# Keys by four heads with both signs, partly DMA-transposed LN1 and one-input statistics in a conditioned linear-attention block

## Chip, cores and metric

The kernel runs on one core of one Trainium2 chip. The metric is the device time of one execution in microseconds (us); every ratio here uses runs of the fast state alone. The runs come from three chips, so across chips the ratio to the kernel before on the same chip is the safer comparison. PE is the matrix engine (TensorE), DVE VectorE, ACT ScalarE, POOL GpSimd, SP the engine that issues most DMAs. LN1 and LN2 are the two layer norms.

## The reference

2048 tokens of width 512 pass a conditioned layer norm, linear attention with 32 heads of width 16, whose features are two softmaxes (of the projected vector and of its negative), and then a second layer norm and a gated MLP (F = 1376).

```python
mod = (silu(c) @ w_mod).reshape(1, 6, 1, -1)              # sa, ca, ga, sb, cb, gb
h = layernorm(x) * (1 + ca) + sa
q, k, v = split(h @ wqkv)                                  # 32 heads of 16
pq, pk = q @ w_phi, k @ w_phi                              # per head, 16x16
phi_q = concat(softmax(pq), softmax(-pq))                  # 32 features per head
phi_k = concat(softmax(pk), softmax(-pk))
kv = einsum('bhsf,bhsd->bhfd', phi_k, v);  z = phi_k.sum(tokens)
o = (phi_q @ kv) / (phi_q @ z + 1e-6)
x = x + ga * (o @ wo)
h = layernorm(x) * (1 + cb) + sb
x = x + gb * ((sigmoid(h @ w_gate) * (h @ w_up)) @ w_down)
```

## The kernel before

Tokens come in 16 tiles of 128. The kernel has its own list scheduler: each piece of work names its engines, buffers, a due time and sometimes a release time, and the schedule is computed when the kernel is built. The due times are hand-set constants.

LN1, with `mv1` holding mean and variance, `rs1` the reciprocal deviation and `nmr` = -mean x rs1:

```python
# two inputs in SBUF: mean and rs of 1 or 2 tiles at once
dve.scalar_tensor_tensor(nmr[:, 0, sl], mv1[:, sl, 0], -1.0, rs1[:, sl], op0=ALU.mult, op1=ALU.mult)
...
def f_xn(e, t=t, xn=xn):                       # normalize one tile, on the engine that the scheduler chose
    if e == "ACT":
        act.activation(xn[:], x_sb[:, t, :], ACT.Identity, scale=rs1[:, t:t + 1], bias=nmr[:, 0, t:t + 1])
    elif e == "DVE":
        dve.tensor_scalar(xn[:], x_sb[:, t, :], mv1[:, t, 0:1], rs1[:, t:t + 1], op0=ALU.subtract, op1=ALU.mult)
    else:
        pool.tensor_scalar(xn[:], x_sb[:, t, :], rs1[:, t:t + 1], nmr[:, 0, t:t + 1], op0=ALU.mult, op1=ALU.add)
...
pe.transpose(tp[:, tl * P:(tl + 1) * P], xn[:, j * P:(j + 1) * P], ident[:])   # 64 of these
dve.tensor_scalar(dst, tp[:], modc[:, 4 + j:5 + j], modc[:, j:j + 1], op0=ALU.mult, op1=ALU.add)  # or ACT: h1T
```

The key/value stage, per tile: K and V on PE, two exponentials on ACT (`e`), sums and reciprocals (`ks`, DVE or ACT), `phi` = e x 1/sum on POOL, the cast of V to `vaug` on ACT, then the sum over tokens:

```python
for g in range(NG):                            # 8 groups: one sign, 8 heads, 136 columns
    s, blk = g // 4, g % 4
    pe.matmul(acc[g // 3][:, (g % 3) * 136:(g % 3) * 136 + 136],
              lhsT=ph[...][:, s, blk * 8:(blk + 1) * 8, :], rhs=vaug[va.slot][:, blk * 8:(blk + 1) * 8, :], ...)
```

At the end of the stage, DVE multiplies the sums by a block mask into `kvbd`. The queries, output projection, LN2 and MLP follow.

Of the kernel before, what the change touches and what calls it, by code (L numbers as in the profile page):

```python
# [10 lines left out]
BF16 = mybir.dt.bfloat16  # L11
# [18 lines left out]
SPLIT = 14  # L30
T0, KP, GL = 11.57, 2.64, 7.92
WARM = [3.5, 3.8, 4.1, 4.4, 4.7, 5.0, 5.3, 5.6, 5.9, 6.2, 7.0, 7.6, 8.2, 8.8, 9.4, 10.0]
LG = [[0], [1], [2, 3], [4, 5], [6, 7], [8, 9], [10, 11], [12, 13], [14, 15]]
QREL = [43.49, 61.34, 57.73, 11.53]
AREL = [-41.36, 49.26, 40.7, 68.7, 71.54, 83.02, 104.54, 113.86, 145.92]
RS1 = [{"ACT": 0.4}] * 3 + [{"POOL": 1.1, "ACT": 0.4}] * 6
XN1 = [
    ['ACT'], ['ACT', 'DVE'], ['ACT'], ['ACT', 'POOL'], ['POOL'], ['DVE', 'ACT', 'POOL'], ['POOL', 'DVE', 'ACT'], ['ACT'], ['DVE'],
    ['POOL', 'DVE'], ['POOL', 'DVE'], ['DVE', 'POOL'], ['DVE', 'ACT'], ['POOL'], ['ACT', 'POOL'], ['ACT', 'DVE', 'POOL'],
# [3 lines left out]
    [['DVE', 'ACT'], ['DVE'], ['ACT'], ['ACT', 'DVE']], [['ACT', 'DVE'], ['DVE'], ['ACT'], ['DVE']], [['DVE'], ['DVE', 'ACT'], ['ACT'], ['ACT']],  # L43
    [['DVE', 'ACT'], ['DVE'], ['DVE'], ['ACT', 'DVE']], [['ACT', 'DVE'], ['DVE', 'ACT'], ['DVE'], ['DVE']],
    [['DVE'], ['DVE'], ['DVE', 'ACT'], ['ACT', 'DVE']], [['DVE', 'ACT'], ['DVE'], ['DVE', 'ACT'], ['DVE']],
    [['DVE'], ['DVE', 'ACT'], ['DVE'], ['DVE', 'ACT']], [['ACT'], ['DVE', 'ACT'], ['DVE'], ['ACT']],
]
RK = [
    ['DVE'], ['DVE', 'ACT'], ['ACT'], ['DVE'], ['DVE', 'ACT'], ['DVE'], ['ACT', 'DVE'], ['DVE', 'ACT'], ['ACT', 'DVE'], ['DVE'], ['ACT', 'DVE'],
    ['ACT', 'DVE'], ['ACT', 'DVE'], ['DVE', 'ACT'], ['DVE', 'ACT'], ['ACT', 'DVE'],  # L50
]
KD = [24.54, 22.76, 2.76, 26.45, -4.23, -2.7, 7.22]
LGD = [-1.87, 20.88, 6.63, 17.49, 10.73, 11.29, 6.86, 2.4, -12.64]
GSL = [6.72, 0.31, 0.38, 0.42, -0.41, 12.03]
UD = [-1.91, -6.06, -6.9, -5.31, 0.39, 2.19, -4.99, -8.58, -4.71]
MISC = [26.51, 50.04, 52.97, 56.98, 1.23, 5.02]
WDREL, WDDUE, WDSTEP = 78.45, 153.49, 1.05
# [25 lines left out]
class Graph:  # L83
# [5 lines left out]
    def __init__(self, caps):  # L89
        self.caps = dict(caps)  # L90
        self.tasks = []
        self.writer, self.readers = {}, {}

    def add(self, name, alts, fn, r=(), w=(), bufs=(), due=1e6, rel=0.0, nbytes=0, port=("POOL",)):
        t = Task(name, alts, fn, due, rel, list(bufs), nbytes, port)
        for k in r:
            if k in self.writer:
                t.deps.add(self.writer[k])
            self.readers.setdefault(k, []).append(t)
        for k in w:  # L100
            if k in self.writer:
                t.deps.add(self.writer[k])
            for q in self.readers.get(k, ()):
                if q is not t:
                    t.deps.add(q)
            self.writer[k] = t
            self.readers[k] = []
        for b in t.bufs:
            b.users += 1
        self.tasks.append(t)  # L110
        return t

    def order(self):
# [5 lines left out]
        for t in reversed(self.tasks):  # L119
            for q in t.succ:  # L120
                t.due = min(t.due, q.due - (3.0 if q.nbytes else min(q.alts.values())) - self.LAT)
        free_at = {e: 0.8 for e in ("PE", "ACT", "DVE", "POOL", "SP")}
# [9 lines left out]
        while left:  # L132
# [16 lines left out]
            for t in list(ready):  # L149
# [25 lines left out]
                if t.nbytes < 0:  # L175
                    t.end = now + 2.5
# [33 lines left out]
def kernel(  # L210
# [22 lines left out]
    bmask = cst.tile([P, P], BF16, name="bmask")  # L233
    modc = cst.tile([P, 16], FP32, name="modc")
# [34 lines left out]
    x_v = A_x.flatten_outer_dims().rearrange("(p n) d -> p n d", n=NT)  # L269
    o_v = out.flatten_outer_dims().rearrange("(p n) d -> p n d", n=NT)  # L270
# [4 lines left out]

    with nc.allow_non_contiguous_dma(reason="small w_phi load"):
        pool.dma_start(wp_sb[:], A_w_phi.rearrange("(kt hl) d f -> (hl d) kt f", hl=8))
    act.preload_act_table_set("natural_log_exp_and_others")
    act.dma_start(c_row[:], c)
# [6 lines left out]
                       pattern=[[DH, 8], [0, DH]], channel_multiplier=-1)  # L286
    pool.memset(mhalf[:], -0.5)
# [29 lines left out]

    def kv_tasks(G, acc, t, ph, va, due, chain=()):
        def kv(e):
            for g in range(NG):  # L320
                s, blk = g // 4, g % 4
                pe.matmul(acc[g // 3][:, (g % 3) * 136:(g % 3) * 136 + 136],  # L322
                          lhsT=ph[:].rearrange("p (s h j) -> p s h j", s=2, j=DH)[:, s, blk * 8:(blk + 1) * 8, :].rearrange("p h j -> p (h j)"),
                          rhs=vaug[va.slot][:, blk * 8:(blk + 1) * 8, :].rearrange("p h d -> p (h d)"),
                          start=(t == 0 and g % 3 == 0), stop=(t == NT - 1), skip_group_check=True)
        G.add(f"kv{t}", {"PE": 0.47}, kv, r=[("phi", t), ("phi", t, 0), ("phi", t, 1), ("vaug", t)], w=["kvacc", *chain], bufs=[ph, va] + acc, due=due)

    def kvbd_tasks(G, acc):
        for i in range(3):
            ng = 3 if i < 2 else 2  # L330

            def f(e, i=i, ng=ng):
                src = acc[i][:, 0:ng * 136].rearrange("p (g h c) -> p g h c", h=8, c=VC)
                dve.tensor_tensor(kvbd[:, 3 * i:3 * i + ng, 0:P].rearrange("p g (h d) -> p g h d", d=DH), src[:, :, :, 0:DH],
                                  bm.unsqueeze(1).to_broadcast([P, ng, 8, DH]), op=ALU.mult)

            def f2(e, i=i, ng=ng):
                src = acc[i][:, 0:ng * 136].rearrange("p (g h c) -> p g h c", h=8, c=VC)
                dve.scalar_tensor_tensor(kvbd[:, 3 * i:3 * i + ng, P:P + 8], src[:, :, :, DH], 0.5e-6,
                                         bm[:, :, 0].unsqueeze(1).to_broadcast([P, ng, 8]), op0=ALU.add, op1=ALU.mult)  # L340
            G.add(f"kvz{i}", {"DVE": 0.17}, f2, r=["kvacc", "bmask"], w=[("kvz", i)], bufs=[acc[i]])
            G.add(f"kvn{i}", {"DVE": 0.18 * ng}, f, r=["kvacc", "bmask"], w=[("kvn", i)], bufs=[acc[i]])
# [3 lines left out]
    def downstream(G, eT, base, first):  # L346
# [18 lines left out]
        for p, tiles in enumerate(UNITS):  # L365
# [98 lines left out]
            if on_act:  # L464
                G.add(f"nmr2_{p}", {"DVE": 0.16}, lambda e, sl=sl: dve.scalar_tensor_tensor(nmr[:, 1, sl], mv2[:, sl, 0], -1.0, rs2[:, sl], op0=ALU.mult, op1=ALU.mult),  # L465
                      r=[("rs2", p)], w=[("nmr2", p)], due=d0 + 1)
            if first and p == 0:
                G.add("tsw", {"ACT": 1.5}, lambda e: act.preload_act_table(ACT.Tanh),
                      r=[("rs2", 0)] + [("kr", t, a) for t in range(NT) for a in range(2)], w=["tsw"], due=d0 + 3)
# [41 lines left out]
        for k in range(NC):  # L511
# [23 lines left out]
            for tl in range(CHUNKS[k]):  # L535
                y = bank("y_ps")
                t = C0[k] + tl
                for ft in range(FT):
                    fsz = P if ft < FT - 1 else F_LAST

                    def f_y(e, k=k, tl=tl, ft=ft, fsz=fsz, y=y):
                        pe.matmul(y[:], lhsT=hm_all[:fsz, hm[k].slot, ft, tl * P:(tl + 1) * P], rhs=wd_sb[:fsz, ft, :], start=(ft == 0), stop=(ft == FT - 1))  # L542
                    i = tl * FT + ft
                    due = gdue[k + 1, i * FT // nd] + 0.02 if k + 1 < NC else ydue + i * 0.216
                    G.add(f"y{t}.{ft}", {"PE": 0.216}, f_y, r=[("hm", k, ft), ("wd", ft)], w=[("y", t)] + ([("ycap", t % 2)] if ft == 0 else []), bufs=[hm[k], y], due=due)
                ot = Buf("ot", [P, D], BF16, "ot")

                def f_fin(e, t=t, y=y, ot=ot):
                    if first and t == NT - 1:
                        load_flag()  # L550
                    dve.tensor_tensor(ot[:], y[:], x1[t][:], op=ALU.add)  # L551
                G.add(f"fin{t}", {"DVE": 0.69}, f_fin, r=[("y", t), ("ycap", t % 2)], w=[("ot", t)], bufs=[y, x1[t], ot], due=due + 1.0)
                G.add(f"st{t}", {"SP": 0.1}, lambda e, t=t, ot=ot: sp.dma_start(o_v[:, t, :], ot[:]), r=[("ot", t)], w=[("out", t)], bufs=[ot], due=due + 2.0, nbytes=128e3)
# [33 lines left out]
    G = Graph(CAPS)  # L587
# [34 lines left out]
    def f_c3(e):  # L622
# [9 lines left out]
        bm.unsqueeze(1).to_broadcast([P, KT, 8, DH]), op=ALU.mult), w=["bd"], due=-20.0, rel=5.0)  # L632
# [80 lines left out]
    for g, ts in enumerate(LG):  # L713
# [18 lines left out]
        nmr_used = any(e != "DVE" for t in ts for e in XN1[t])  # L732
        if nmr_used:
            G.add(f"nmr1_{g}", {"DVE": 0.16}, lambda e, sl=sl: dve.scalar_tensor_tensor(nmr[:, 0, sl], mv1[:, sl, 0], -1.0, rs1[:, sl], op0=ALU.mult, op1=ALU.mult),
                  r=[("rs1", g)], w=[("nmr1", g)], due=gd)
        for t in ts:
# [3 lines left out]
            def f_xn(e, t=t, xn=xn):  # L740
# [4 lines left out]
                else:  # L745
                    pool.tensor_scalar(xn[:], x_sb[:, t, :], rs1[:, t:t + 1], nmr[:, 0, t:t + 1], op0=ALU.mult, op1=ALU.add)
            alts = {e: XN1_T[e] for e in XN1[t]}
            G.add(f"xn1_{t}", alts, f_xn, r=[("rs1", g)] + ([("nmr1", g)] if set(alts) != {"DVE"} else []), w=[("xn1", t)],
                  bufs=[xn], due=gd, port=("POOL", "DVE"))
        for j in range(KT):  # L750
# [206 lines left out]
```

## Time and profile before

| kernel before | |
|---|---|
| time, median of 3 runs | 227.13 us (226.31 to 227.37) |
| span of the profiled run, mean granted clock | 224.9 us, 0.986 |
| PE, DVE, ACT, POOL busy | 93%, 74%, 48%, 39% |

A busy PE is not a PE at its peak, since ends of matmuls are modelled and overlap. I therefore count PE's work from the built order at the measured spacing, as the prediction shows; what an elapsed stretch has beyond that work is called "lost". Two more rows of this profile: the first is from the groups by form (output <- inputs, partitions x elements, count, busy us, mean ns of one, idle before). The second is from the table by stretch, for 8 to 58 us, which is most of the key/value stage (busy us of each engine, instructions in brackets, then granted clock, DMA share and GB/s).

```profile
L746 POOL TENSOR_SCALAR xn<-x_sb,rs,nmr 128x512 bf16<-128x512 bf16 x8 | 6.2, 772 | 8.1 <-DVE nmr L734 7.9
```

```profile
core 0: us, PE busy (x) PEld busy (x) DVE busy (x) ACT busy (x) POOL busy (x), PEclk, DMA share, GB/s
8.00:58.00 50.00, 44.35 (x387) 26.33 (x390) 45.93 (x89) 39.54 (x90) 34.13 (x30) 0.97 0.59 205
```

POOL has 16 us of slack in these 50, DVE 4.

### The profile page before, as it was taken

The numbers are of one execution on the slowest core, as the hardware profiler recorded it, in microseconds if no ns is written. First come the engines' busy times: TensorE is split into PE (matmuls) and PEld (weight loads), VectorE is DVE, ScalarE is ACT, GpSimd is POOL, SyncE is SP. The second block draws the span as 40 slices with busy tenths as digits, with TensorE's granted clock in tenths as the row PEclk, the third lists the DMA queues.
The fourth block names the chain that finished last, engine by engine and source line by source line (L and its number), as shares of the span: only waits on it lengthen the run. The fifth ranks groups of instructions, "written<-read, shape, count | busy, mean of one in ns | idle before, by whom it ended". The sixth has DMA issues, their size and how long they took to land.

```text
span 224.9 us, 4268 instructions
## 1 busy us (share of the span) xinstructions
PE 210.1 (93%) x1558; PEld 118.9 (53%) x1580; DVE 165.5 (74%) x366; ACT 107.6 (48%) x233; POOL 87.0 (39%) x99
## 2 busy tenths in 40 slices
PE   7987979889999998999999999999999999999980
PEld 2634545555466658787775444555444444444430
DVE  2599997998828999988869698699999844433230
ACT  3689857978959885633452324622214413322100
POOL 5236969776985199944304041122401100000000
PEclk9999979999999999999999999999999999999997
DMA  6973899500000020253160211413201130000011
GB/s 191 356 298 81 292 394 389 161 3 1 0 3 0 3 47 4 48 59 61 38 82 3 70 25 24 86 33 71 47 0 50 48 94 24 3 0 25 26 63 41
DMA packets 26143, 18.23 MB, mean 81 GB/s; under 512 B 17937, under 2 KB 23426, under 8 KB 26114
## 3 DMA queue, kind: packets, MB, share of 16 engines
q1 hardware_dynamic: 26080, 17.86, 27.8%
q8 instruction: 14, 0.23, 0.4%
q14 instruction: 15, 0.12, 0.2%
q0 software_dynamic: 32, 0.02, 0.0%
q10 hardware_dynamic: 2, 0.00, 0.0%
HBM read 11.58 MB, written 2.10 MB: 61 GB/s over the span
## 4 chain that ended last, share of the span: by engine, by line
PE 74%; DVE 19%; issue 3%; ACT 2%; DVEq 0%; ACTq 0%
PE y_ps L542 17%; PE u_ps L522 16%; PE g_ps L522 16%; PE a_ps L440 5%; PE v_ps L781 4%; PE k_ps L777 4%; PE warm L647 3%; DVE st L719 3%; DVE ks L793 2%; PE kvacc L322 2%; PE q_ps L845 2%; PE num L407 2%; DVE u L413 2%; DVE h1T L761 2%; DVE st L449 1%
## 5 line engine op out<-in xcount | busy, mean ns | idle before, releaser
L526 ACT ACTIVATE tg<-g_ps 128x512 bf16<-128x512 f32 (+5 forms) x66 | 29.1, 453 | 70.7 <-PE g_ps L522 60.0
L531 DVE SCALAR_TENSOR_TENSOR wmod_sb<-tg,u_ps 128x512 bf16<-128x512 bf16 (+5 forms) x66 | 32.3, 504 | 23.2 <-PE u_ps L522 22.0
L542 PE MATMUL y_ps<-wd_sb,wmod_sb 128*128 128x512 bf16 (+1 forms) x170 | 44.9, 379 | 0.5 <-ACT tg L526 0.2
L796 POOL TENSOR_TENSOR phi<-e,ks 128x1024 bf16<-128x1024 bf16 (+1 forms) x18 | 31.0, 1735 | 7.5 <-ACT ks L804 2.0
L431 POOL TENSOR_TENSOR o<-u 128x512 bf16<-128x512 f32 x14 | 17.5, 1271 | 40.0 <-DVE u L413 40.0
L522 PEld LDWEIGHTS <-wg_sb 128*128 128x128 bf16 (+1 forms) x264 | 23.6, 100 | 17.2
L522 PEld LDWEIGHTS <-wu_sb 128*128 128x128 bf16 (+1 forms) x264 | 23.6, 100 | 16.7 <-issue 0.8
L522 PE MATMUL u_ps<-wqk_sb,wu_sb 128*128 128x128 bf16 (+3 forms) x175 | 31.0, 298 | 0.7 <-DVE wmod_sb L531 0.6
L522 PE MATMUL g_ps<-wqk_sb,wg_sb 128*128 128x128 bf16 (+3 forms) x173 | 30.8, 297 | 0.2
L542 PEld LDWEIGHTS <-wmod_sb 128*128 128x128 bf16 (+1 forms) x176 | 16.7, 98 | 17.9 <-ACT tg L526 0.4
L413 DVE TENSOR_TENSOR u<-num,cc 128x512 f32<-128x512 f32 (+1 forms) x32 | 20.1, 681 | 0.2
L793 DVE TENSOR_REDUCE ks<-e 128x64 f32<-128x1024 bf16 (+1 forms) x18 | 19.1, 1080 | 0.9 <-ACT e L790 0.9
L781 PE MATMUL v_ps<-wv_sb,h1T 128*128 128x512 bf16 x58 | 17.0, 405 | 1.9 <-DVE h1T L761 1.5
L551 DVE TENSOR_TENSOR ot<-y_ps,x 128x512 bf16<-128x512 f32 x16 | 11.0, 689 | 9.8 <-PE y_ps L542 9.7
L790 ACT ACTIVATE e<-k_ps 128x512 bf16<-128x512 f32 x32 | 17.2, 600 | 2.1 <-PE k_ps L777 1.9
L522 PE MATMUL u_ps<-wT_sb,wu_sb 128*128 128x256 bf16 (+3 forms) x87 | 17.8, 325 | 0.1
L522 PE MATMUL g_ps<-wT_sb,wg_sb 128*128 128x256 bf16 (+3 forms) x88 | 17.9, 326 | 0.0
L850 ACT ACTIVATE eT<-q_ps 128x512 bf16<-128x512 f32 x32 | 16.7, 621 | 1.4 <-PE q_ps L845 1.4
L777 PE MATMUL k_ps<-wqk_f,h1T 128*128 128x512 bf16 x64 | 16.3, 379 | 0.5 <-ACT h1T L763 0.3
L440 PE MATMUL a_ps<-wo_sb,oT 128*128 128x512 bf16 x61 | 15.1, 379 | 0.2
L845 PE MATMUL q_ps<-h1T,wqk_f 128*128 128x512 bf16 x63 | 14.7, 379 | 0.1
L479 ACT ACTIVATE xn<-x,nmr,rs 128x512 bf16<-128x512 f32 x14 | 10.7, 805 | 4.9 <-DVE nmr L465 4.9
(115 smaller groups left out, 282.0 us busy)
## 6 DMA issues: line engine op xcount, KB each, us to landing
wmod_sb<-in_w_mod_dram SPq DMA_DIRECT2D x1, 2048.0 KB, 8.4
out_dram<-ot SPq DMA_DIRECT2D x16, 128.0 KB, 1.9
x_sb<-in_A_x_dram SPq DMA_DIRECT2D x3, 512.0 KB, 9.3
wg_sb<-in_B_w_gate_dram SPq DMA_DIRECT2D x1, 1376.0 KB, 12.3
wu_sb<-in_B_w_up_dram SPq DMA_DIRECT2D x1, 1376.0 KB
wd_sb<-in_B_w_down_dram SPq DMA_DIRECT2D x1, 1280.0 KB, 16.6
wqk_sb<-in_A_wqkv_dram SPq DMA_DIRECT2D x2, 512.0 KB, 4.6
wmod_sb<-in_w_mod_dram SPq DMA_DIRECT2D x2, 512.0 KB, 6.2
```

What stands on the lines that cost most here:

```text
L413: dve.tensor_tensor(u[:], ps[:].rearrange("p (h d) -> p h d", d=DH), cc[:, q, s, :].unsqueeze(2).to_broadcast([P, H, DH]), op=ALU.mult)
L431: G.add(f"o{t}", {"POOL": 1.3}, lambda e, ub=ub, o=o: pool.tensor_tensor(o[:], ub[0][:].rearrange("p h d -> p (h d)"), ub[1][:].rearrange( ...
L440: pe.matmul(ap_[:], lhsT=oT[:, j, :], rhs=wo_sb[:, j, :], start=(j == 0), stop=(j == KT - 1))
L522: pe.matmul(ps[:fsz, 0:n], lhsT=w[:, j, ft * P:ft * P + fsz], rhs=h[:, j, 0:n], start=(j == 0), stop=(j == KT - 1))
L526: G.add(f"tg{k}.{ft}", {"ACT": 0.13 + n * 0.00083}, lambda e, tg=tg, g_ps=g_ps, fsz=fsz, n=n: act.activation(tg[:fsz, 0:n], g_ps[:fsz, 0:n ...
L531: dve.scalar_tensor_tensor(hm_all[:fsz, hm[k].slot, ft, 0:n], tg[:fsz, 0:n], 1.0, u_ps[:fsz, 0:n], op0=ALU.add, op1=ALU.mult)
L542: pe.matmul(y[:], lhsT=hm_all[:fsz, hm[k].slot, ft, tl * P:(tl + 1) * P], rhs=wd_sb[:fsz, ft, :], start=(ft == 0), stop=(ft == FT - 1))
L777: pe.matmul(kp[:], lhsT=h1T[:, j, t * P:(t + 1) * P], rhs=wqk_f[:, j, D:2 * D], start=(j == 0), stop=(j == KT - 1))
L781: pe.matmul(vp[:], lhsT=h1T[:, j, t * P:(t + 1) * P], rhs=wv_sb[:, j, :], start=(j == 0), stop=(j == KT - 1))
L793: dve.tensor_reduce(ks[:, a:b], ee[:, a:b], axis=AX.X, op=ALU.add)
L796: engine(e).tensor_tensor(ph[:].rearrange("p (s h j) -> p s h j", s=2, j=DH)[:, a:b], ee[:, a:b], ks[:, a:b].unsqueeze(3).to_broadcast([P, ...
L845: pe.matmul(qp[:], lhsT=wqk_f[:, j, blk * P:(blk + 1) * P], rhs=h1T[:, j, cq * 512:(cq + 1) * 512], start=(j == 0), stop=(j == KT - 1))
```

## The change

The intent: fewer columns for the key/value sum (a head's own block is a quarter of each product, not an eighth), fewer PE transposes, no two-input DVE instruction that can meet POOL at the SBUF port, and a shorter tail. Cut to its core:

```diff
-SPLIT = 14
+NPART = [1, 1, 1, 1, 1, 1, 1, 1, 1, 1, 1, 1, 2, 1, 2, 4]      # phi of the last tiles in parts
 ... all hand-set due and release times, and the engines each step may take, were set anew ...
+TD = [0, 0, 1, 0, 0, 0, 1, 1, 0]                               # groups that go by DMA transpose (6 tiles)
 ...
-x_v = A_x.flatten_outer_dims().rearrange("(p n) d -> p n d", n=NT)
+x_v = A_x.flatten_outer_dims().rearrange("(n p) d -> p n d", p=P)          # the output likewise
-pool.dma_start(wp_sb[:], ...)
+act.dma_start(wp_sb[:], ...)
 ... LN1 (the same change of nmr was made in LN2) ...
-dve.scalar_tensor_tensor(nmr[:, 0, sl], mv1[:, sl, 0], -1.0, rs1[:, sl], op0=ALU.mult, op1=ALU.mult)
+for t in ts:
+    dve.tensor_scalar(nmr[:, 0, t:t + 1], mv1[:, t, 0:1], rs1[:, t:t + 1], -1.0, op0=ALU.mult, op1=ALU.mult)
-    pool.tensor_scalar(xn[:], x_sb[:, t, :], rs1[:, t:t + 1], nmr[:, 0, t:t + 1], op0=ALU.mult, op1=ALU.add)
+    pool.tensor_scalar(xn[:], x_sb[:, t, :], mv1[:, t, 0:1], rs1[:, t:t + 1], op0=ALU.subtract, op1=ALU.mult)
+if TD[g]:   sp.dma_start_transpose(h1T[:, :, t * P:(t + 1) * P], xn[:])     # then modulate h1T in SBUF, in place
 ... key/value sum: 8 groups of 4 heads x both signs, 68 columns ...
+pe.matmul(acc[g // 4][:, (g % 4) * HC:(g % 4 + 1) * HC], lhsT=ph[:, g * P:(g + 1) * P],
+          rhs=vaug[va.slot][:, 4 * g:4 * g + 4, :], ...)
-G.add(f"va{t}", {"ACT": 0.61}, ...)
+G.add(f"va{t}", {"ACT": 0.51, "DVE": 0.6}, ...)                             # the cast of V may go to DVE
 ... at the end: kvm = acc x mask (DVE), kvp = bd^T kvm (16 PE matmuls), copies to kvbd (DVE, ACT) ...
 ... the last y tile in two halves of 256 columns, each with its own store ...
```

## The prediction

> **What bounds the kernel now.** I read the page's totals and its 40 slices first, to see which engine fills the span and where it does not.
>
> ```profile
> PE 210.1 (93%) x1558; PEld 118.9 (53%) x1580; DVE 165.5 (74%) x366; ACT 107.6 (48%) x233; POOL 87.0 (39%) x99
> ...
> PE   7987979889999998999999999999999999999980
> ...
> DVE  2599997998828999988869698699999844433230
> ...
> POOL 5236969776985199944304041122401100000000
> PEclk9999979999999999999999999999999999999997
> ```
>
> PE is full from slice 10 (56 us) to the last y matmul. In slices 1 to 8 DVE is nearly full and PE is not, and POOL is at 6 to 9 from slice 4 on. In slice 5 the granted clock falls to 7 tenths: the starved PE also lost clock there.
>
> Busy PE is not PE at its peak, so I counted PE's work instead. Spacing from start to start comes from the chain of waits and the timeline: 8 matmuls of 512 columns in 1.73 us (216 ns), 16 of 128 columns in 0.89 us (56 ns), 32 of 136 columns in 1.89 us (59 ns); 32 of 16 columns start inside 0.80 us (26 ns). With these the built program's PE order holds 203.6 us of matmuls. The first starts at 1.25, the last ends at 218.74: 217.5 us. So 13.9 us are lost, and where tells the bound:
> - first Q group: work before it 44.7, elapsed 56.7 (starts at 57.98), loss 12.0;
> - first y: work 75.8, elapsed 89.3 (90.55), loss 13.5;
> - last y: loss 13.9.
>
> After 90 us PE alone sets the time; all but 0.4 us of the loss is earlier, and 12.0 of it lies in the key/value stage. There the chain of waits runs through DVE:
>
> ```profile
> 20.79 1.10 DVE ks L793
> 21.90 0.96 DVE h1T L761 x3
> 22.85 0.46 DVE ks L806
> 23.31 1.08 DVE ks L793
> 24.39 1.01 DVE nmr L734
> 25.40 1.14 DVE ks L793
> 26.57 0.55 DVE ks L806
> 27.12 1.08 DVE nmr L734
> ...
> 43.90 1.54 DVE xn L744
> ...
> 62.47 1.89 PE kvacc L322 x32
> ...
> 92.46 0.89 PE num L407 x16
> ```
>
> An instruction on two numbers per partition (nmr) takes over 1 us there. The view of that source line has its minimum, median and maximum:
>
> ```profile
> L734 DVE SCALAR_TENSOR_TENSOR nmr<-mv,rs x9: 96/150/1612, 6.3 to 46.5; 128x2 f32<-128x2 f32 x7, 128x1 f32<-128x1 f32 x2
> ```
>
> The long ones lie over POOL's phi (1929 ns each). The groups by form give what the change touches:
>
> ```profile
> L796 POOL TENSOR_TENSOR phi<-e,ks 128x1024 bf16<-128x1024 bf16 x14 | 26.9, 1929 | 7.5 <-ACT ks L804 2.0 <-DVE nmr L734 1.7 <-DVE ks L806 1.6
> L322 PE MATMUL kvacc<-vaug,phi 128*128 128x136 bf16 x128 | 9.7, 223 | 0.3 <-POOL phi L796 0.2
> L756 PE MATMUL tp_h<-ident,xn 128*128 128x128 bf16 x64 | 6.3, 219 | 1.7 <-POOL xn L746 0.5 <-DVE h1T L761 0.5 <-DVE xn L744 0.3
> ```
>
> **What the Trainium skill says.** "SBUF — State Buffer", Who interferes with whom: a DVE instruction with two SBUF inputs contends with a GpSimd instruction that reads SBUF, the loser waiting for the whole instruction; one with at most one SBUF input and outside the 2-port modes does not. The trace agrees: nmr has two inputs and spreads from 96 to 1612 ns, the one-input ks reduction beside it stays near 1198. "TensorE: Matmul & The Clock Gate", Wait — 56ns, not 53.3ns?: N/2.4 + 2.5 ns from start to start, never under about 25. The trace has 59 at N=136 and 26 at N=16, so N=68 should run at 31. The same page, Back-to-back issue gap, has 81 ns for N=128 with a weight load each; this trace has 56, so the measurement decides. "DMA: Bandwidth & Descriptors", Specifications: 512 B is enough for line rate; x in row order comes in pieces of 1 KB, so I charge nothing for it beyond 0.1 us, though no run here shows it yet.
>
> **The change part by part.** Groups of 4 heads with both signs: a head's own block is then a quarter of the product instead of an eighth, and each of the 128 matmuls streams 68 columns instead of 136. PE: 128 x (59 - 31) ns = -3.6 us. New at the end: two mask multiplications on DVE (some 0.4 us each, estimated from kvbd's 417 ns at 256 columns), 16 permuting matmuls (16 x 31 ns = +0.5 us of PE), then the copies. The accumulator's three kvn products become copies, one on ACT, so DVE gets about 0.5 us more. The path from the last key block to the sums grows by a mask, a matmul group and two hand-overs, about 1 us; the built order leaves Q groups around it, but only 4 matmuls (0.86 us) between the permutation and the sums, so I charge +0.6 us.
>
> LN1: 6 of 16 tiles go by DMA transpose. PE loses 24 of 64 transposes: 24 x 56 ns = -1.3 us. Their modulation becomes 12 instructions out of SBUF: in the built order 6 on ACT, 4 on POOL, 2 on DVE (these two can meet the port wait that xn had at 43.90). The four-head layout also splits the last tiles' work into halves and quarters.
>
> PE's sum, counted over the whole built order: 203.6 to 199.1, -4.5 us (-3.6 + 0.5 - 1.3, the rest rounding and short matmuls).
>
> DVE in the key/value stage, before and after: nmr 4.7 us (7 of 627 ns and 2 of 138) to 15 one-input pieces at about 0.1 = 1.5; xn 2.3 (3 of 762) to 0, as none stays on DVE; modulation about 1.5 less; the vaug copy, new on DVE for 7 tiles in the built order, 7 x 0.65 = +4.6; reductions +0.5 and reciprocals -0.6; weight copies -0.4. Net -2.9 us, and what goes is mostly waiting on the listed chain (1.01 + 1.08 + 1.54).
>
> POOL in the same stage: phi as before, 31 us; xn 11 instead of 8, +2.3; 4 modulations at some 0.45, +1.8; mask and permutation +1.5. About +5 us, while the load of w_phi leaves its queue (-1.0 at the start, hidden).
>
> The tail: the last y tile in two halves shortens the last DVE addition from 0.69 to about 0.38, and the last store is half as long: -0.4 us. Stores otherwise lie beside PE's work and give nothing.
>
> Sum on the path: PE -4.5, tail -0.4, kvbd path +0.6, and the loss in the key/value stage. For that I take -2.5 from DVE's relief and from the clock not dropping in slice 5 (two slowed slices cost about 1.3 us: 5.6 x 0.25), and +1.2 from POOL below. Total -5.6: 227.13 - 5.6 = **221.5 us**.
>
> **The rivals.** (1) POOL becomes the bound. From the first phi (18.52) to the end of the last (65.27) it has about 39 us of work and 7.5 idle. Afterwards that stretch holds some 42.5 us. If it idles as much, the last phi ends 3 us later than now, Q groups run out before the sums, and the gain shrinks to about 2.5: 224.5. For it: slices at 9 up to 62 us. Against it: POOL's idle time was waiting for ACT and DVE (2.0 + 1.7 + 1.6), which the change feeds earlier. I count it at under half, hence +1.2.
> (2) The DMA transposes arrive late. A transpose lands 2.4 us after issue, and the first two stand in one queue behind the last x and wq loads, with DMA at 0.96 of its share between 8 and 16 us. If tiles 2 and 3 miss their slot near 17 us, PE idles 1 to 2 us and the clock may drop again: 223.
> (3) DVE really was the limit to 48 us: then all its freed waits come back as PE work, loss falls by 5, and the time is 218 to 219. Against it: the 4.6 us of vaug copies moved there.
> (4) The rearranged schedule hides nothing and only PE's -4.5 and the tail's -0.4 count: 222.2.
>
> **Range and chances.** 2% faster is 222.6. The middle (221.5) and rivals 3 and 4 are under it, 1 and 2 over it, 4 only just under. I give rivals 1 and 2 together about a third. Slower by 2% needs a new stall of 10 us, which nothing in the built order suggests. Range 217.8 to 225.0; faster 0.62, same 0.34, slower 0.04.
>
> **What would show it.** Right: kvacc groups of 8 at about 0.25 us instead of 0.47; no nmr over 0.3 us; granted clock at 9 in slice 5; less than 12 us lost before the first Q group; still under 1 us lost after the first y. Wrong: POOL's last phi after 65 us and PE waiting for kvacc or kvp (rival 1); PE idle before 20 us with DMA transposes as the releaser (rival 2); 68-column matmuls still at 55 ns or more, which would take 3 us of gain away; x landing later than before.

## The result, and the profile after

The changed kernel gives the right output, but it takes 235.72 us (median of 4, 235.49 to 236.87), against 227.25 us for the kernel before beside it (226.31 to 227.75). A ratio here and below is the mean time of one kernel's fast runs over that of the other's of the same rounds, so not quite the ratio of the quoted medians. It is 1.039 (95% interval 1.034 to 1.044): slower by 3.9%, where I had expected it faster by 2.5%.

The page of the changed kernel, totals and slices (slices are tenths busy, 40 over the span; here 5.8 us each):

```profile
PE 208.6 (89%) x1559; PEld 115.8 (50%) x1583; DVE 163.9 (70%) x380; ACT 108.6 (46%) x247; POOL 107.9 (46%) x115
...
PE   7694793897899997999999998999999999999990
...
POOL 4759999999999829785110044200004510000000
```

POOL's total went from 87.0 to 107.9 us, and its row is full from slice 3 to slice 12; PE's holes are now there too. The same table by stretch as shown of before:

```profile
8.00:58.00 50.00, 36.43 (x311) 19.84 (x313) 35.98 (x78) 36.51 (x87) 46.62 (x32) 0.93 0.63 190
```

POOL is busy 46.6 of 50 us, 12.5 more than before, while PE fell by 7.9, DVE by 10.0 and ACT by 3.0. From its first `phi` to the end of its last, at 20.6 and 73.2 us, POOL is busy 51.8 of 52.6 us: it sets the pace of this stage. Which group of POOL grew is in the groups by form:

```profile
L875 POOL TENSOR_TENSOR phi<-e,ks 128x1024 bf16<-128x1024 bf16 x13 | 25.0, 1927 | 0.3
L812 POOL TENSOR_SCALAR xn<-x_sb,mv,rs 128x512 bf16<-128x512 bf16 x12 | 24.9, 2076 | 3.1 <-ACT rs L790 2.7
L893 DVE CAST vaug<-v_ps 128x512 bf16<-128x512 f32 x7 | 4.8, 682 | 1.7 <-PE v_ps L857 1.4 <-PE kvacc L343 0.2
```

`phi` is unchanged. `xn` took 772 ns of POOL before; it takes 2076 now, for the same tile in the same type. Its inputs are now x, mv, rs. Twelve of them are 24.9 us instead of 6.2. The waits of the changed kernel (engine and line, what released it, us in total, times, longest) show that the others wait for it, mostly through `phi`, which stands behind `xn` in POOL's queue:

```profile
PEld L343 <- POOL phi L875: 11.2, 10, 4.5
...
PE kvacc L343 <- POOL phi L875: 8.2, 8, 4.0
ACT e L869 <- POOL phi L875: 6.7, 2, 4.2
...
PE tp_h L826 <- POOL xn L812: 3.5, 3, 2.0
```

PE and PEld report the same wait twice, so these must not be added. One such stretch in the chain of waits (start us, us, what):

```profile
23.09 1.89 POOL phi L875
24.99 2.06 POOL xn L812
...
34.45 0.87 POOL phi L875
35.31 1.89 POOL xn L812
37.34 3.81 POOL phi L875 x2
41.23 1.94 POOL phi L875
43.21 1.54 PE kvacc L343 x24
```

The last `phi` ends at 73.2 us (before: 65.3), the first Q group starts at 64.6 (57.98), the first y matmul at 101.1 (90.5). The counted work before that y is 73.5 us, so 26.3 are lost by then instead of 13.5. From there to the last y about 1.5 us more are lost (0.4 before).

### The profile page after: what moved, and what is told of

It reads as the page before. It is cut to its first block, busy times and chain, and to the rows that moved or that the text cites. A ratio compares the mean times of both kernels' runs of the same rounds, so it can differ in the third digit from the quotient of the medians.

```text
span 233.8 us, 4338 instructions
## 1 busy us (share of the span) xinstructions
PE 208.6 (89%) x1559; PEld 115.8 (50%) x1583; DVE 163.9 (70%) x380; ACT 108.6 (46%) x247; POOL 107.9 (46%) x115
## 4 chain that ended last, share of the span: by engine, by line
PE 51%; POOL 16%; issue 10%; DVE 10%; ACT 9%; DMA 2%; POOLq 0%; DVEq 0%; ACTq 0%; SPq 0%
PE y_ps L604 14%; PE g_ps L581 13%; PE u_ps L581 13%; POOL phi L875 7%; POOL xn L812 6%; PE a_ps L496 4%; ACT e L869 3%; PE warm L710 3%; DVE u L469 2%; DMA oT<-o 2%; ACT eT L932 2%; DVE st L505 1%; DVE x L501 1%; PE num L463 1%; PE k_ps L853 1%
## 5 line engine op out<-in xcount | busy, mean ns | idle before, releaser
L604 PE MATMUL y_ps<-wd_sb,wmod_sb 128*128 128x512 bf16 (+2 forms) x180 | 43.7, 366 | 0.3
L875 POOL TENSOR_TENSOR phi<-e,ks 128x1024 bf16<-128x1024 bf16 (+2 forms) x21 | 31.4, 1512 | 0.5
L581 PEld LDWEIGHTS <-wu_sb 128*128 128x128 bf16 (+1 forms) x264 | 23.5, 100 | 15.7
L581 PE MATMUL g_ps<-wT_sb,wg_sb 128*128 128x512 bf16 (+3 forms) x130 | 26.7, 325 | 0.2
L581 PE MATMUL u_ps<-wT_sb,wu_sb 128*128 128x512 bf16 (+3 forms) x130 | 26.6, 325 | 0.1
L872 DVE TENSOR_REDUCE ks<-e 128x64 f32<-128x1024 bf16 (+2 forms) x21 | 19.6, 952 | 9.8 <-POOL phi L875 5.2
L812 POOL TENSOR_SCALAR xn<-x_sb,mv,rs 128x512 bf16<-128x512 bf16 x12 | 24.9, 2076 | 3.1 <-ACT rs L790 2.7
L869 ACT ACTIVATE e<-k_ps 128x512 bf16<-128x512 f32 (+2 forms) x42 | 17.7, 507 | 10.0 <-POOL phi L875 6.7
L581 PE MATMUL g_ps<-wqk_sb,wg_sb 128*128 128x128 bf16 (+5 forms) x132 | 22.1, 290 | 0.1
L581 PE MATMUL u_ps<-wqk_sb,wu_sb 128*128 128x128 bf16 (+5 forms) x131 | 21.9, 290 | 0.1
L613 DVE TENSOR_TENSOR ot<-y_ps,x 128x512 bf16<-128x512 f32 (+1 forms) x17 | 11.2, 657 | 11.1 <-PE y_ps L604 11.1
## 6 DMA issues: line engine op xcount, KB each, us to landing
wd_sb<-in_B_w_down_dram SPq DMA_DIRECT2D x1, 1280.0 KB, 13.5
```

What stands on the lines that cost most here:

```text
L581: pe.matmul(ps[:fsz, 0:n], lhsT=w[:, j, ft * P:ft * P + fsz], rhs=h[:, j, 0:n], start=(j == 0), stop=(j == KT - 1))
L604: pe.matmul(y[:, 0:c1 - c0], lhsT=hm_all[:fsz, hm[k].slot, ft, tl * P:(tl + 1) * P], rhs=wd_sb[:fsz, ft, c0:c1], start=(ft == 0), stop=(ft ...
L812: pool.tensor_scalar(xn[:], x_sb[:, t, :], mv1[:, t, 0:1], rs1[:, t:t + 1], op0=ALU.subtract, op1=ALU.mult)
L869: act.activation(ee[:, ha:hb, s, :], kp[:, ha * DH:hb * DH].rearrange("p (h j) -> p h j", j=DH), ACT.Exp, scale=1.0 - 2.0 * s)
L872: dve.tensor_reduce(ks[:, ha:hb].rearrange("p h s -> p (h s)"), ee[:, ha:hb].rearrange("p h s j -> p (h s) j"), axis=AX.X, op=ALU.add)
L875: pool.tensor_tensor(ph[:, ha * 32:hb * 32].rearrange("p (h j) -> p h j", j=DH), ee[:, ha:hb].rearrange("p h s j -> p (h s) j"), ks[:, ha: ...
```

## The experiments

Fourteen kernels were run. The table has the losses ahead of the first y matmul for those that the argument uses: counted PE work ahead of it, its start, and the difference less the 1.25 us at which PE starts. Times and ratios are over all runs; the last three columns are from one profiled run each.

| kernel | time, us (median) | ratio to before | work to first y | first y at | lost |
|---|---|---|---|---|---|
| before (medians beside the others) | 226.6 to 227.4 | 1 | 75.8 | 90.5 | 13.5 |
| changed | 235.72 | 1.039 | 73.5 | 101.1 | 26.3 |
| e1, changed, multiply-add | 224.31 | 0.991 | 73.5 | 89.9 | 15.2 |
| e2, before, subtract-multiply | 230.03 | 1.012 | 75.8 | 94.0 | 17.0 |
| e5, changed, add(-mean) | 225.83 | 0.998 | 73.5 | 91.9 | 17.1 |
| e7, before, one-input | 224.08 | 0.987 | 75.8 | 88.0 | 11.0 |
| e9, e5 with small casts | 223.74 | 0.985 | 73.5 | 90.1 | 15.3 |
| e13, e7 and four heads | 222.24 | 0.980 | 73.8 | 86.7 | 11.7 |

**The theory** after the trace: the POOL form alone made the change slow. **Rivals**: POOL waits for something that makes the instruction long (a port held by DVE, or data), or the rest of the change is at fault (transposes, grouping, the new order).

### e1: the changed kernel with the old form on POOL

```diff
-pool.tensor_scalar(xn[:], x_sb[:, t, :], mv1[:, t, 0:1], rs1[:, t:t + 1], op0=ALU.subtract, op1=ALU.mult)
+pool.tensor_scalar(xn[:], x_sb[:, t, :], rs1[:, t:t + 1], mv1[:, t, 0:1], op0=ALU.mult, op1=ALU.add)
```

> The changed kernel with only the two operations and operands of GpSimd's xn exchanged (multiply by rs, add the mean: a wrong value on purpose, same waits, same order of every instruction). Theory A (GpSimd's subtract-then-multiply form is slow by itself, 2.07 us against 0.77, and GpSimd is the bound of the key/value stage): xn falls to about 0.77 us, GpSimd loses 12 x 1.3 = 15.6 us of work, its last phi ends near 60 to 64 us instead of 73, the kernel takes 220 to 225 us. Theory B (xn is long because of its mean operand or of contention with DVE, or the time was lost to the DMA transposes and the new order): xn stays over 1.5 us, or falls and the time stays above 230 us.

The same buffers, dependencies and order on every engine; the output is wrong (relative error 0.024). Measured: 224.31 us (ratio 0.991, 0.986 to 0.995). From the groups by form:

```profile
L812 POOL TENSOR_SCALAR xn<-x_sb,rs,mv 128x512 bf16<-128x512 bf16 x12 | 9.2, 769 | 4.4 <-ACT rs L790 4.1
```

11.4 us of time (11.0 by the ratios) go with 15.7 us of POOL work, and the last `phi` ends at 62.0 instead of 73.2, all as theory A expected. So the grouping, the transposes and the order cannot be what made the kernel slower than before. They didn't bring the predicted 5.6 us either.

### e2: the new form in the kernel before

```diff
-pool.tensor_scalar(xn[:], x_sb[:, t, :], rs1[:, t:t + 1], nmr[:, 0, t:t + 1], op0=ALU.mult, op1=ALU.add)
+pool.tensor_scalar(xn[:], x_sb[:, t, :], mv1[:, t, 0:1], rs1[:, t:t + 1], op0=ALU.subtract, op1=ALU.mult)
```

> The kernel before with only GpSimd's xn turned into subtract the mean, multiply by rs (right values, same order). Theory A: its 8 xn go from 0.77 to 2.07 us, 10.4 us more GpSimd work against 7.5 us of idle time there, so the kernel gets 3 to 8 us slower (230 to 235). Theory B: xn stays near 0.77 us and the time at 227.

Measured: 230.03 us (1.012, 1.010 to 1.015), with right values and the same order. The 8 instructions took 16.6 us instead of 6.2:

```profile
L746 POOL TENSOR_SCALAR xn<-x_sb,mv,rs 128x512 bf16<-128x512 bf16 x8 | 16.6, 2079 | 5.6 <-ACT rs L727 5.6
```

10.4 us of new POOL work cost only 2.8 us, just under the 3 to 8 that theory A gave. POOL had slack here: in the kernel before it idled 8.1 us ahead of `xn` and 7.5 ahead of `phi`. The 12 slow ones of the changed kernel cost 11.4: with the slack used up, some seven tenths of POOL's added time went into the result.

### e3: POOL alone

A small kernel: it loads x once and then runs `tensor_scalar` of a 128x512 bf16 tile on POOL in several forms, while no other engine works. Its output is wrong, which doesn't matter for the time.

> Nothing but GpSimd operations with two per-partition numbers on 128x512 tiles, one form after another, no other engine at work (the output is not the reference's, on purpose). Theory A: multiply-add 0.77 us, subtract-multiply 2.07 us with nothing to contend with; if it is the subtraction, multiply-subtract and the single subtraction are slow too; if only the pair multiply-add is fast, add-multiply is slow as well. Theory B: all forms near 0.77 us.

Groups by form; m and r are scalars per partition. L25 is multiply then add, L27 subtract then multiply, L29 add then multiply, L33 subtract alone, L35 multiply alone:

```profile
L27 POOL TENSOR_SCALAR y<-x,m,r 128x512 bf16<-128x512 bf16 x2 | 4.1, 2077 | 0.0
L33 POOL TENSOR_SCALAR y<-x,m 128x512 bf16<-128x512 bf16 x2 | 3.1, 1568 | 0.0
L35 POOL TENSOR_SCALAR y<-x,r 128x512 bf16<-128x512 bf16 x2 | 3.1, 1571 | 0.0
L29 POOL TENSOR_SCALAR y<-x,m,r 128x512 bf16<-128x512 bf16 x2 | 1.5, 774 | 0.0
L25 POOL TENSOR_SCALAR y<-x,r,m 128x512 bf16<-128x512 bf16 x2 | 1.5, 772 | 8.3 <-DMA x<-in_A_x_dram 8.3
```

The length belongs to the form, not to contention: 2077 ns with DVE idle. Multiply-multiply took 782 ns and multiply-subtract 2082. Whether the scalars are the same or different doesn't matter (2085), and subtracting and multiplying by immediates takes 1932. With 256 columns, subtract-multiply takes 1232 ns and multiply-add 559, so most of the difference grows with the columns: 3.3 against 0.83 ns per column. The surprise is L33 and L35: one operation takes twice as long as two. Which pairs of multiply, add and subtract are quick is measured here; why they are isn't shown.

The Trainium skill, "GPSIMD Engine Reference", Elementwise — side-by-side cycle accounting, has 512 elements at its best rate in 768 ns predicted and 769 measured. The quick pairs agree (772); nothing there tells which operations reach that rate, and Engine selection calls one-input work "roughly line-rate", which 2077 and 1568 ns do not fit: DVE did the same 128x512 normalization in 316 ns at the least in the kernel before.

### e4: a repair that reorders

```diff
-nmr_used = any(e == "ACT" for t in ts for e in XN1[t])
+nmr_used = any(e != "DVE" for t in ts for e in XN1[t])
-pool.tensor_scalar(xn[:], x_sb[:, t, :], mv1[:, t, 0:1], rs1[:, t:t + 1], op0=ALU.subtract, op1=ALU.mult)
+pool.tensor_scalar(xn[:], x_sb[:, t, :], rs1[:, t:t + 1], nmr[:, 0, t:t + 1], op0=ALU.mult, op1=ALU.add)
```

> The changed kernel with a right repair: GpSimd's xn is again multiply by rs, add the negative of mean times rs, and waits for that number again (which moves the scheduled order). Theory A: 219 to 225 us, faster than both kernels if the other parts are worth what the prediction gave them (221.5). Theory B: above 230 us.

A miss: 237.9 us (1.047), though `xn` is back at 768 ns. POOL's tiles now depend on `nmr`, and with that dependency the scheduler built another order. POOL multiplies `wo` while `phi` is still due. Timeline of POOL (start us, us, engine line op):

```profile
54.27 2.29 POOL L911 TENSOR_TENSOR wo_sb<-wo_sb,ga_sb 128x512 bf16<-128x512 bf16 x2
56.63 3.93 POOL L875 TENSOR_TENSOR phi<-e,ks 128x1024 bf16<-128x1024 bf16 x2
```

The last `phi` ends at 70.1, where e1's ended at 62.0. The hand-set times had been made for the other graph. `xn` and the order both changed here, so this run cannot tell what the form is worth, and the repair had to keep the order.

### e5: a repair that keeps the order

```diff
+dve.tensor_scalar(negm[:, t:t + 1], mv1[:, t, 0:1], -1.0, None, op0=ALU.mult)     # right after the statistics, POOL tiles only
-pool.tensor_scalar(xn[:], x_sb[:, t, :], mv1[:, t, 0:1], rs1[:, t:t + 1], op0=ALU.subtract, op1=ALU.mult)
+pool.tensor_scalar(xn[:], x_sb[:, t, :], negm[:, t:t + 1], rs1[:, t:t + 1], op0=ALU.add, op1=ALU.mult)
```

> The changed kernel with GpSimd's 12 normalizations as add(-mean), then multiply by rs; the negated mean is 12 more pieces of about 60 ns on DVE, right after each tile's statistics, so no new dependency crosses engines and the built order is the changed kernel's own plus these pieces. Right values, unlike the earlier multiply-add run. Theory (the form of the GpSimd normalization alone makes the change slow): 224 to 226 us, ratio to the kernel before 0.985 to 0.995, xn at about 775 ns. Rival (the multiply-add run was fast for another reason, or any disturbance of DVE costs much): over 229 us.

Right values; 225.83 us (0.998, 0.993 to 1.002), 9.9 us below the changed kernel (9.4 by the ratios); the time is as expected, the ratio just above its range. From the groups by form:

```profile
L816 POOL TENSOR_SCALAR xn<-x_sb,negm,rs 128x512 bf16<-128x512 bf16 x12 | 9.1, 767 | 4.6 <-ACT rs L794 4.3
```

It is 1.5 us slower than e1, which has another quick form and lacks the 12 small DVE pieces; they took 154 ns each, 1.8 us, not the 60 ns that I had expected. That difference is barely clear of the noise (1.6 us by the ratios, whose intervals overlap), so the pieces' part in it is not shown. So the form is the cause of the slowdown, and what is left is as fast as the kernel before, with 4.5 us less counted PE work. The next runs ask where that went.

### e6: the key/value sum issued twice

```diff
-for g in range(a, b):
+for g in [g for g in range(a, b) for _ in range(2)]:       # numerator and denominator both double
```

> The same as the run with add(-mean), but every one of the 128 matmuls that sum the keys with the values is issued twice, so numerator and denominator double and the result hardly changes. 128 more matmuls of 68 columns are about 4.0 us of TensorE work (31 ns each), about what the four-head grouping was to take away (3.6 us). If this TensorE work lies on the path that sets the end, as my prediction had it: 3 to 4.5 us slower than the run without the doubling. If the key/value stage is set by GpSimd and DVE and TensorE's work there lies beside theirs: under 1.5 us slower, and then the term of 3.6 us in my sum was mostly hidden time.

228.6 us (1.008, 1.004 to 1.011) against e5's 225.83 on the same chip: 2.8 us for 4.0 us of added PE work, 2.2 by the ratios, in the same order otherwise. With the two intervals combined that is some 1 to 3.5 us. It falls between the two expectations. PE's work in this stage counts, at some six tenths (a quarter to nine tenths by that interval); it is neither hidden nor, as it seems, the sole bound.

### e7 and e8: single parts in the kernel before

e7 has only the one-input `nmr`, with the order unchanged:

```diff
-dve.scalar_tensor_tensor(nmr[:, 0, sl], mv1[:, sl, 0], -1.0, rs1[:, sl], op0=ALU.mult, op1=ALU.mult)
+for t in ts:
+    dve.tensor_scalar(nmr[:, 0, t:t + 1], mv1[:, t, 0:1], rs1[:, t:t + 1], -1.0, op0=ALU.mult, op1=ALU.mult)
```

> The kernel before with only the nmr instruction of LN1 changed from one two-input instruction per group to one-input pieces per tile (two multiplications by numbers per partition); same order on every engine. My prediction gave the relief of DVE in the key/value stage, of which these waits are the largest part (7 of them at 627 ns), up to 2.5 us. If DVE's waits there set the end: 1.5 to 3 us faster than the kernel before. If DVE only moves its waiting elsewhere, because GpSimd's phi comes no earlier: within 1 us.

224.08 us (0.987, 0.984 to 0.990): 2.9 us faster for three lines, the upper end of the first expectation. The view of that line (count: minimum/median/maximum ns):

```profile
L736 DVE TENSOR_SCALAR nmr<-mv,rs x16: 114/203/205, 6.3 to 43.8; 128x1 f32<-128x1 f32 x16
```

No piece is over 205 ns, where the two-input form had reached 1612. The granted clock stays at 1.00 from 24 to 40 us; in the profiled run of the kernel before it was 0.93 from 24 to 32 us and 0.86 from 32 to 40. That clock does not look like the source of the gain: of the 43 fast runs of the kernel before, the 20 with a mean clock of 0.99 or more took 227.1 us on average, the 20 between 0.98 and 0.99 took 226.7.

e8 has only the tokens in row order:

```diff
-x_v = A_x.flatten_outer_dims().rearrange("(p n) d -> p n d", n=NT)
+x_v = A_x.flatten_outer_dims().rearrange("(n p) d -> p n d", p=P)          # and o_v
```

> The kernel before with only the assignment of tokens to tiles changed to row order (x is read and the result stored in pieces of 1 KB per partition at larger strides; same order on every engine). I charged 0.1 us for it. Expected: within 0.7 us of the kernel before; x's first tile lands some 0.5 us sooner or later. If the layout of x in DRAM is worth more than that: over 1 us either way.

226.84 against 226.99 us (1.001, 0.998 to 1.005): no effect, as predicted.

### e9 and e10: lightening what the change added

Both start from e5, keep its order, and are wrong. e9 cuts DVE's 7 casts of V:

```diff
-dve.tensor_copy(vaug[va.slot][:, :, 0:DH], vp[:]...)
+dve.tensor_copy(vaug[va.slot][:, 0:4, 0:DH], vp[:, 0:4 * DH]...)
```

> The repaired kernel (add(-mean) on GpSimd) with each of DVE's 7 casts of a value tile cut from 512 columns to 64, wrong on purpose; same order on every engine. It takes away most of the 4.8 us that the change newly put on DVE in the key/value stage. If that added DVE work is where TensorE's 4.5 us went: 2 to 3.5 us faster than the repaired kernel, so 222.5 to 224. If GpSimd alone sets the stage: under 1 us.

```profile
L897 DVE CAST vaug<-v_ps x7: 164/216/227, 17.2 to 59.2; 128x64 bf16<-128x64 f32 x7
```

223.74 us (0.985, 0.980 to 0.989), 2.1 us below e5 (3.0 by the ratios), as the first expectation had it. The casts took 7 x (680 - 205) ns = 3.3 us less of DVE, with 205 their mean. Not all of that was freed: DVE's two modulations out of SBUF rose from 1.5 to 3.2 us; the longer one, 2.8 us, ran beside POOL's `xn` and `phi`. And POOL's four settings of `vaug` took 2.0 us in place of 0.6, since e9 has to set the whole tile once. So DVE is close to setting this stage, and the casts look like a good part of what ate the gain.

e10 cuts the 12 modulations out of SBUF:

```diff
+if tp is None: dst = dst[:, 0:64]
```

> The repaired kernel with the 12 modulations of the tiles that came by DMA transpose (6 on ACT, 4 on GpSimd, 2 on DVE) done on 64 of 256 columns, wrong on purpose; same order on every engine. It takes about 1.6 us from GpSimd, 1 us from ACT and up to 1 us from DVE. If GpSimd sets the stage: 1 to 2.5 us faster than the repaired kernel, so 223.5 to 225. If DVE or TensorE do: under 1 us.

226.07 us (0.994, 0.989 to 0.999): not told apart from e5. POOL's four went from 553 to 394 ns only, so they freed 0.6 us of POOL and not 1.6. DVE's two rose from 1.5 to 3.1 us; both started while a `phi` was running, where in e5 one did. So DVE had no relief at all. The run is a weak test.

### e11: two-input statistics back in the repaired kernel

```diff
-for t in ts:
-    dve.tensor_scalar(nmr[:, 0, t:t + 1], mv1[:, t, 0:1], rs1[:, t:t + 1], -1.0, op0=ALU.mult, op1=ALU.mult)
+dve.scalar_tensor_tensor(nmr[:, 0, sl], mv1[:, sl, 0], -1.0, rs1[:, sl], op0=ALU.mult, op1=ALU.mult)
```

> The repaired kernel with the two-input nmr instruction of the kernel before in LN1; right values, same order on every engine. In the kernel before, one-input pieces gave 2.9 us. If they do the same in the changed kernel: 1.5 to 3.5 us slower than the repaired kernel, so 227.3 to 229.5, and the other parts of the change alone would then be slower than the kernel before. If the slack differs there: within 1 us.

226.11 us (0.995, 0.990 to 0.999): no loss against e5, so the second expectation. The groups by form say why:

```profile
L802 DVE SCALAR_TENSOR_TENSOR nmr<-mv,rs 128x2 f32<-128x2 f32 x7 | 1.9, 264 | 0.0
```

In this order only one of the seven pieces lies over a `phi`, and that one took 0.55 us: 264 ns on average, against 627 in the kernel before, where three lay inside a `phi` and took 1.1 to 1.6 us. A part that gives 2.9 us in one schedule gives nothing that these runs can see in another.

### e12: the cheap parts together

The kernel before with one-input pieces in both normalizations and the last y tile in two halves; nothing in the key/value stage moves.

```diff
+cuts = [(0, 256), (256, 512)] if t == NT - 1 else [(0, 512)]     # and the nmr pieces of e7, in LN1 and LN2
```

> The kernel before with one-input pieces for nmr in both normalizations and the last output tile in two halves: the parts of the change that cost no other engine work. Right values; the scheduler moves a few late instructions near the end, nothing before LN2. Against 224.1 us with the pieces in LN1 alone: the halves should give 0.3 to 0.5 us, so 223.3 to 224.3, faster than both kernels. Rival: the late instructions that moved cost the tail as much: over 224.3.

225.01 us (0.992, 0.986 to 0.997), a miss: not better than e7 with the LN1 pieces alone, and not clearly worse, as the intervals overlap. The smaller tail was not seen; the scheduler also moved y and gate matmuls, so the halves alone stay unmeasured.

### e13 and e14: the two PE parts apart

e13 is e7 with the grouping by four heads, the mask and the permutation; no DVE casts, no DMA transposes, the due times of the kernel before. The scheduler reorders it.

```diff
+pe.matmul(acc[g // 4][:, (g % 4) * HC:(g % 4 + 1) * HC], lhsT=ph[:, g * P:(g + 1) * P], rhs=vaug[va.slot][:, 4 * g:4 * g + 4, :], ...)
+... kvm, kvp, copies to kvbd, as in the change; nmr as in e7 ...
```

> The kernel before with one-input nmr pieces (224.1 us alone, PE's work 203.6 us) and of the rest of the change only the grouping by 4 heads and both signs with the permutation: TensorE's work 200.4 us, no casts on DVE, no DMA transposes. If TensorE's saving counts in this kernel: 221.5 to 223 us. If the longer hand-over at the end (mask, permutation, copies) and the new order eat it: 223.5 to 226.

Right values, and 222.24 us (0.980, 0.977 to 0.983): faster than every other right kernel here, 4.3 us below the kernel before and 1.8 below e7 (1.6 by the ratios, whose intervals just fail to meet). Since the order changed too, the 1.8 us are those of grouping and new order together. The timeline of PE has one tile's 8 products and two tiles' 16 (start us, us):

```profile
47.05 0.42 PE L328 MATMUL kvacc<-vaug,phi 128*128 128x68 bf16 x8
49.90 0.67 PE L328 MATMUL kvacc<-vaug,phi 128*128 128x68 bf16 x16
```

The second 8 take 0.25 us, 31 ns each, as predicted. And the stretch from 8 to 58 us is fuller than before on PE and on POOL, at clock 1.00:

```profile
8.00:58.00 50.00, 46.52 (x421) 25.88 (x418) 44.56 (x98) 43.92 (x101) 41.11 (x38) 1.00 0.60 205
```

e14 is e5 with all transposes back on PE (`TD` all 0), rescheduled.

> The repaired change with all LN1 transposes back on TensorE: its work 200.5 instead of 199.1 us, modulations from PSUM again, no transpose waits for a DMA; rescheduled. If the DMA transposes are worth their 1.3 us of TensorE: 1 to 2 us slower than the repaired kernel's 225.8. If they cost more by SBUF-to-SBUF modulations and late landings than they save: 1 to 3 us faster, 223 to 225.

236.2 us (1.041), outside both expectations. Its first Q group starts at 54.6, earlier than e5's 55.9, and the loss comes later, around 92 us, where PE waits for the first tiles of LN2 (waits between 80 and 104 us):

```profile
PE tp_x L554 <- DVE xn L541: 2.1, 1, 2.1
```

The granted clock is 0.68 from 88 to 96 us. That is a schedule that doesn't fit the set times, like e4, and no verdict on DMA transposes.

## Why the prediction was wrong

**The step that failed** is the size of POOL's term: "xn 11 instead of 8, +2.3", which made "About +5 us" of POOL work and +1.2 on the path. It priced the new instruction at the 0.77 us of the row for multiply-add, although the diff changes the operation to subtract-multiply on that engine. Measured: 12 of them at 2076 ns, 24.9 instead of 6.2 us, so +18.7 in place of +2.3 (e3: 2077 ns alone). That one term is worth 9.9 us (e5), or 11.4 (e1); by the ratios 9.4 or 11.0. It is most, not all, of the 14 us between forecast and result. No row of the kernel before had this form on POOL; it existed on DVE alone. The honest entry would have been "unpriced", with its own branch of the range.

**The rival was named, and too small.** Rival 1 (POOL becomes the bound) has the right mechanism: the last `phi` after 65 us and PE waiting for `phi` before `kvacc` are what the trace shows. It was held to 3 us because its size came from the same wrong price: it gave POOL 42.5 us of work from the first `phi` to the last, and the trace has 51.8. (Its 224.5 also counts POOL twice: the 3 us are added to a total that already holds +1.2, without which it is 223.3.) "Slower by 2% needs a new stall of 10 us, which nothing in the built order suggests" fell with it: the built order named the new operation, but the price had been taken by engine and shape.

**PE's sum was right, its worth only in part.** The 68-column spacing is 31 ns (e13). But e6 puts PE's work in this stage at some six tenths of its size, and e13 finds 1.8 us for the grouping with its new order, where I had -3.6, +0.5 and +0.6, so -2.5.

**DVE's relief of -2.5 was right for another kernel.** In the kernel before, `nmr` alone gives 2.9 us (e7). In the changed one, it gives nothing that the noise lets through (e11). I had taken 1.5 us for the 15 one-input pieces; they were busy for 2.4. And cutting the casts moved to DVE (7 x 0.68 us) gave 2 to 3 us of time (e9), which the sum had netted away as busy time. The part for the clock is not borne out: runs of the kernel before with a higher mean clock are no faster (figures at e7). Its working was off too: 5.6 x 0.25 is one slowed slice, not two, and DVE's row has only 5 in slice 1, which I called nearly full. DVE's total did not fall: 165.5 us before, 166.0 in e5.

**Right**: no `nmr` over 0.3 us (213 ns at most), x in row order (e8), and against rival 2, no wait for a transpose that came by DMA in the trace of the changed kernel before 70 us. Wrong besides: 22.4 us are lost before the first Q group instead of under 12 (40.9 us of counted work ahead of it), about 1.5 us after the first y instead of under 1, and the clock did not stay up: PE's 4.0 us wait before 41.2 us is followed by 0.57 from 40 to 48 us.

**Open**: what the DMA transposes are worth (e14 doesn't say), what the tail halves are worth (e12), and the rest of e5's loss beyond the casts. e5 loses 17.1 us ahead of the first y and e13 11.7; casts (e9) account for 2 to 3 us, and the repair's own DVE pieces (e1 against e5, barely clear of noise) perhaps for 1.5; they may overlap, and the rest is open.

## What to carry to other kernels

Price an instruction by its engine, its operations and its form together; where the profile has no row of that combination, measure it alone before trusting a sum (e3 needs one small kernel). A relief on one engine is worth what its schedule makes of it, so test a part in the order in which it will run. Here the best kernel came from taking two parts of the change and leaving the rest: the one-input statistics and the grouping, 222.2 us, 2.0% below the kernel before.

## What the Trainium skill lacked or had wrong

- "GPSIMD Engine Reference": the cost of a tensor_scalar depends on its pair of operations, and the page doesn't say so. 128x512 bf16: multiply-add, add-multiply and multiply-multiply 772 to 782 ns; subtract-multiply and multiply-subtract 2077 to 2082; one operation alone 1568 to 1571. Its Engine selection has one-input work at roughly line rate, which the forms at 1568 to 2082 ns do not fit.
- "SBUF — State Buffer", Who interferes with whom: agrees, and could add a size. Two-input pieces of 2 elements averaged 627 ns and reached 1612 in one schedule and averaged 264 in another; one-input pieces stayed at or under 214. The two-input pieces that took 1.1 to 1.6 us lay inside a POOL instruction of 1.9 us. A DVE modulation of 128x256 from SBUF to SBUF, with one SBUF input, took 338 ns at least and 2281 at most in e1; the page allows for that only in its 2-port modes, and no run here shows the mode.
- "TensorE: Matmul & The Clock Gate", Back-to-back issue gap: 81 ns for N=128 with a weight load each is not what these kernels show (56 ns); 68 columns, also with a weight load each, took 31 ns.
